# Gates turned and spread over the adapter ranks through DRAM, so that the down projection of the middle chunks is made transposed

## The chip, the cores and the metric

The kernel runs on one NeuronCore of one Trainium2 chip. The metric is the device time of one execution in microseconds. A core has TensorE (PE), which multiplies matrices into PSUM; VectorE (DVE), ScalarE (ACT) and GpSimd (POOL) for elementwise work; SyncE (SP), which issues transfers; and 16 DMA engines that all queues share.

## The reference

Two stages are computed, attention over a pooled key grid and then a mixture of eight small adapters on its output:

```
kv_pool = kv.reshape(B, H/4, 4, W/4, 4, C).mean(axis=(2, 4))   # B 4, C 128: 768 keys a batch
k = v = kv_pool.reshape(B, -1, C) @ w_sr
a = softmax((q @ k.T) / sqrt(C));  x = a @ v                    # q: 12288 rows a batch
logits = x @ w_gate                                             # 8 experts
top 2 of 8 -> softmax over the two -> w
out = x + sum over the two experts e of  w_e * (x @ A[e]) @ B[e]   # rank 16
```

All eight experts are computed for every row: eight experts of rank 16 are 128 columns, and experts that weren't chosen have gate 0. With two chosen experts the softmax is a sigmoid of the difference of logits, which the kernel makes with a tanh; the factor of one half is folded into A.

## The kernel before, in words

**Tiling.** The 4 x 12288 query rows are cut into 96 chunks of T = 512 rows (24 per batch, `NB`); a chunk is S = 4 blocks of 128 rows. Groups of four chunks (`GC`) share one load of queries: `cast_q` (L79) casts 2048 rows to bf16 in DRAM on GpSimd's queue, `load_qT` (L84) reads them back transposed on the sync queue.

**One chunk** goes through these steps, each a function of its own:

- `scores` (L311): for r = 0, 1, 2 two matmuls of 512 columns into a two-bank PSUM tile `sg`, then one exponential on ScalarE (L319) to `em` in fp16. The pool of `sg` has two buffers.
- `attend` (L321): for each of the four row blocks six matmuls of 137 columns into `acc`: 128 value columns, 8 gate logits (w_gate is folded into the values) and the sum of the exponentials. `acc` has one buffer.
- `normalize` (L331): reciprocal and product on VectorE give `xn`.
- `top` (L362) and `route` (L371): the eight sorted logits on VectorE; differences and mask on GpSimd. Chunks are routed in pairs (`sizes`).
- `gates` (L389): a tanh on ScalarE, a product and a sum on GpSimd give `gw`.
- `transposes` (L398): turns `xn` of one chunk and the gated activations `hg` of another by matmul with the identity, four matmuls each, into one tile `tt_ps`; one copy on VectorE takes both out (L416).
- `down` (L422): four matmuls per chunk with the turned x as weights and A (`a_bf`) as the moving operand give rows by (expert, rank).
- `gate` (L427): VectorE multiplies by the gate of the row and expert, read 16 times over along the rank, into `hg`.
- `up` (L436): four matmuls with the turned `hg` as weights; `finish` (L441): VectorE adds `xn`, and the sync queue stores.

**Order.** The order on every engine is the program's order. Chunks up to 13 and the stretch from chunk 72 on follow order strings written out by hand; slots 14 to 71 come from `slot(k)` (L646). In slot k the kernel computes scores of chunk k, attends for k-1, normalizes k-2, gates k-4 (once per pair), runs the down projection of k-6, turns x of k-6 and `hg` of k-7, and finishes k-8. The slot's core in the code:

```
o.append(f"sc {k} 0")
...
o += [f"nm {k - 2}", f"tt {k - 6} {k - 7} V", f"sc {k} 1", f"up {k - 8}", f"fi {k - 8}",
      f"at {k - 1} 0", f"tp {k - 2}"]
...
o += [f"sc {k} 2", f"dn {k - 6}", f"ge {k - 6}"]
```

**Keys of the next batch.** `load_kv` loads 12 pieces of 512 KB per batch in 12 slots running, GpSimd adds them up (`pa`), and nine steps (`pr`: keys, values, turn, for each third) bring them to `kfT` and `vx`. `next_cast` (L605) first makes GpSimd touch the last query tile that was loaded, so that a cast starts after that load.

**PSUM.** `sg` takes two banks in each of its two buffers, `acc` takes two, and the other products (`tt_ps`, `h_ps`, `d_ps`, the keys' tiles) share a pool of two banks called mb.

Of the kernel before, what the change touches and what calls it, by code (L numbers as in the profile page):

```python
# [20 lines left out]
def kernel(  # L21
# [10 lines left out]
    nc = tc.nc  # L32
    P = 128
    B, N, C = q.tensor.shape
    E, RK = 8, 16
# [3 lines left out]
    T = 512  # L39
    S = T // P  # L40
    GC = 4
# [7 lines left out]
    const = ctx.enter_context(tc.tile_pool(name="const", bufs=1))  # L49
# [6 lines left out]
    rpool = ctx.enter_context(tc.tile_pool(name="rpool", bufs=4))  # L56
    gpool = ctx.enter_context(tc.tile_pool(name="gpool", bufs=6))
    run = ctx.enter_context(tc.tile_pool(name="run", bufs=3))
    opool = ctx.enter_context(tc.tile_pool(name="opool", bufs=6))
    qdram = ctx.enter_context(tc.tile_pool(name="qdram", bufs=1, space=bass.MemoryType.DRAM))  # L60
    ps_s = ctx.enter_context(tc.tile_pool(name="ps_s", bufs=2, space=bass.MemoryType.PSUM))
    ps_a = ctx.enter_context(tc.tile_pool(name="ps_a", bufs=1, space=bass.MemoryType.PSUM))
# [2 lines left out]
    keep = tc.keep_in_program_order  # L65

    def mm(*a, **k):
        return keep(nc.tensor.matmul(*a, **k))  # L68

    def mtile(shape, dtype=FP32, name="mb"):  # L70
        return ps_m.tile(shape, dtype, tag="mb", name=name)


    NG = N // GT
# [48 lines left out]
    for item in """  # L123
# [5 lines left out]
        at = [None if x == "-" else int(x) for x in at]  # L129
# [13 lines left out]
    id_f = const.tile([P, P], FP32)  # L143
# [163 lines left out]
    em, acc, xn, xg, srt, gw = {}, {}, {}, {}, {}, {}  # L307
    tts, xT, hgT, hp, hg, dp = {}, {}, {}, {}, {}, {}
# [34 lines left out]
    def normalize_half(k, h):  # L343
        if ("r", k) not in xn:
            xn["r", k] = rpool.tile([P, S], FP32, tag="rinv", name="rinv")
        if k // GC not in xg:
# [5 lines left out]
            xn[k][:, 2 * h:2 * h + 2], a[:, :, 0:VC],  # L352
            ri.unsqueeze(2).broadcast_to([P, 2, VC]), op=ALU.mult)))

    sizes = [1, 1] + [2] * (NB * (B - 1) // 2 - 1) + [1] * NB
    first, size = {}, {}
    for n in sizes:
        k0 = len(first)
# [3 lines left out]
    def top(k):  # L362
        k0, m = first[k], k - first[k]
        if k0 not in srt:
            srt[k0] = rpool.tile([P, GC, S, 8], FP32, tag="srt", name="srt")
        for s in range(S):
            keep(nc.vector.max(srt[k0][:, m, s], xn[k][:, s, C:VC]))  # L367

# [2 lines left out]
    def route(k0):  # L371
        n = size[k0] * S
        eng = nc.gpsimd
        m0 = k0 % GC * S
        lg = xg[k0 // GC].rearrange("p m s c -> p (m s) c")[:, m0:m0 + n, C:VC]
        so = srt[k0].rearrange("p m s e -> p (m s) e")[:, 0:n]

        def over(i):
            d = rpool.tile([P, GC * S, 8], FP32, tag=f"over{i}", name=f"over{i}")[:, 0:n]
            keep(eng.tensor_tensor(  # L380
                d, lg, so[:, :, i].unsqueeze(2).broadcast_to([P, n, 8]), op=ALU.subtract))
            return d

        arg, mask = over(0), over(1)
        keep(eng.tensor_tensor(arg, arg, mask, op=ALU.add))
        keep(eng.tensor_scalar(mask, mask, 0.0, None, op0=ALU.is_ge))  # L386
        routed[k0] = (n, eng, arg, mask)

    def gates(k0):  # L389
        n, eng, arg, mask = routed[k0]  # L390
        th = rpool.tile([P, GC * S, 8], FP32, tag="th", name="th")[:, 0:n]
        keep(nc.scalar.activation(th, arg, AF.Tanh, bias=0.0, scale=0.5))  # L392
        w = gpool.tile([P, GC * S, 8], FP32, tag="gw", name="gw")
        keep(eng.tensor_tensor(w[:, 0:n], th, mask, op=ALU.mult))  # L394
        keep(eng.tensor_tensor(w[:, 0:n], w[:, 0:n], mask, op=ALU.add))  # L395
        gw[k0] = w
# [30 lines left out]
    def gate(k):  # L427
        k0, m = first[k], k - first[k]
        hg[k] = run.tile([P, S, P], BF16, tag="hg", name="hg")
        keep(nc.vector.tensor_tensor(  # L430
            hg[k].rearrange("p s (e r) -> p (s e) r", e=E),
            hp[k].rearrange("p s (e r) -> p (s e) r", e=E),
            gw[k0][:, m * S:(m + 1) * S].rearrange("p s e -> p (s e)")
            .unsqueeze(2).broadcast_to([P, S * E, RK]), op=ALU.mult))

    def up(k):  # L436
        dp[k] = mtile([P, S, C], name="d_ps")
        for s in range(S):
            mm(dp[k][:, s], hgT[k][:, s], b_bf, start=(s == 0), stop=(s == S - 1))
# [146 lines left out]

    def gates_here(k):
        th, mask = routed[k]
        gw[k] = gpool.tile([P, S, E], FP32, tag="gw1", name="gw1")
        keep(nc.vector.scalar_tensor_tensor(gw[k], th, 1.0, mask, op0=ALU.add, op1=ALU.mult))  # L590

    late = const.tile([P, 1], FP32)
    a_bf = const.tile([P, P], BF16)
    b_bf = const.tile([P, C], BF16)

    def adapters():
        keep(nc.vector.tensor_scalar(a_bf, a_f, 0.5, None, op0=ALU.mult))
        keep(nc.vector.tensor_copy(b_bf, b_f))

    def first_casts(watch):  # L600
        keep(nc.gpsimd.tensor_copy(late, watch))
        for g in range(2, 4):
            cast_q(g)
# [7 lines left out]
    def plan(b):  # L611
# [20 lines left out]
        "nh": normalize_half, "xb": hold_x, "xt": turn_x, "cx": fetch_x, "hb": hold_h, "ht": turn_h, "ch": fetch_h,  # L632
        "o95": hold_acc, "pt": attend_part, "hd": hold_hp, "dn2": down_into, "ge2": gate_part,
        "db": hold_d, "up2": up_part, "af": add_here, "ca": carry, "pd": add_there,
        "lastroute": route_here, "lt": tanh_here, "lg_": gates_here,
    }

    def follow(order):
# [7 lines left out]
    def slot(k):  # L646
        b, i = divmod(k, NB)
        o = []
        if k % GC == 0 and k // GC + 1 < B * NG:
            o.append(f"lq {k // GC + 1}")  # L650
        i0 = 4 if b == 0 else 0
        if b + 1 < B and i0 <= i < i0 + 12:
            o.append(f"kv {b + 1} {(i - i0) // 4} {(i - i0) % 4}")
        if k % GC == 2 and k // GC + 2 < B * NG:
            o.append(f"cq {k // GC + 2}")
        o.append(f"sc {k} 0")
        if first[k - 4] == k - 4:
            o.append(f"ga {k - 4}")
        o += [f"nm {k - 2}", f"tt {k - 6} {k - 7} V", f"sc {k} 1", f"up {k - 8}", f"fi {k - 8}",
              f"at {k - 1} 0", f"tp {k - 2}"]  # L660
        if first[k - 2] + size[k - 2] - 1 == k - 2:
            o.append(f"ro {first[k - 2]}")
        o += [f"sc {k} 2", f"dn {k - 6}", f"ge {k - 6}"]
        prs = (14, 15, 16, 18, 19, 20, 21, 22, 23) if b == 0 else (11, 12, 13, 17, 18, 19, 21, 22, 23)
        if b + 1 < B and i in prs:
            o.append(f"pr {b + 1} {prs.index(i)}")
        o += [f"at {k - 1} {s}" for s in range(1, S)]
        if b + 1 < B and i % 2 == 0 and (8 if b == 0 else 6) <= i <= 20:
            lo, n = ((0, 3, 7, 10, 14, 17, 21)[(i - 8) // 2], 4 if i % 4 else 3) if b == 0 else (
                (i - 6) // 2 * 3, 3)  # L670
            o += [f"pa {b + 1} {m}" for m in range(lo, lo + n)]
        return "; ".join(o)

    follow("""
# [26 lines left out]
    for k in range(14, 72):  # L701
        follow(slot(k))
# [89 lines left out]
```

The softmax here doesn't subtract the row's maximum and nothing guards it: scores larger than these inputs give would overflow.

## Time and profile before

| | |
|---|---|
| time, median of 3 runs | 389.32 us (lowest 388.84) |
| span of the profiled run | 387.5 us, TensorE clock 0.998 |
| PE busy | 378.9 us, 98% |
| VectorE, ScalarE, GpSimd busy | 81%, 80%, 54% |
| moved by DMA | 76.5 MB |
| one exponential (L319), 288 of them | 1026 ns |
| store of one chunk, issue to landing | 3.3 us |
| load of one key piece, issue to landing | 6.2 us |

How to read it: a line of a group has the source line, engine and operation, what is written from what, the shape and the count; after the bar follow busy microseconds, the mean of one in nanoseconds, and the engine's idle time before it with what ended that. A helper records all matmuls, so they all carry L68 and are told apart by their tiles. Matmuls overlap in the pipeline, so the distance between two starts, not the duration, tells what one occupies. In a timeline the columns are start and length in microseconds.

### The profile page before, as it was taken

Reading aid. Unit: us, or ns where it says so; the run is one execution under the profiler, and the core shown is the slowest. Engines: PE = TensorE matmul, PEld = TensorE weight load, DVE = VectorE, ACT = ScalarE, POOL = GpSimd, SP = SyncE. Lnnn points to the kernel's source line nnn. Section 1 sums busy time; section 2 is a strip of 40 time slices with the busy share of each in tenths; the row PEclk is TensorE's granted clock in tenths of the full one; section 3 lists DMA queues with packets and bytes.
Section 4 is the critical chain, followed back from the end, with each engine's and each line's share of the span. In section 5 each row is a group of like instructions: output and inputs, shape, how many; then the busy total and the mean of one; then the engine's idle time right before and its main releaser. Section 6 shows DMA issues by size and latency. Waiting matters only on the chain.

```text
span 387.5 us, 11812 instructions
## 1 busy us (share of the span) xinstructions
PE 378.9 (98%) x4620; PEld 303.8 (78%) x4620; DVE 313.5 (81%) x973; ACT 308.3 (80%) x401; POOL 211.0 (54%) x474
## 2 busy tenths in 40 slices
PE   7899999999999999999999999999999999999994
PEld 4777788888888887888887887888877778788893
DVE  1445688989888888989988889888877687988896
ACT  1688997777687786877788787786879999998964
POOL 0011768987331768777533586877613234545682
PEclk9999999999999999999999999999999999999999
DMA  7998997975596999985579989856745665532245
GB/s 263 413 267 200 295 201 220 285 164 140 136 314 140 255 227 331 234 172 142 119 191 272 305 206 333 200 138 142 156 113 105 128 150 165 111 92 105 81 165 219
DMA packets 70745, 76.47 MB, mean 197 GB/s; under 512 B 49857, under 2 KB 51393, under 8 KB 70337
## 3 DMA queue, kind: packets, MB, share of 16 engines
q1 hardware_dynamic: 69552, 63.98, 55.8%
q0 software_dynamic: 704, 11.54, 17.1%
q8 instruction: 36, 0.59, 0.6%
q10 hardware_dynamic: 432, 0.20, 0.2%
q14 instruction: 21, 0.16, 0.2%
HBM read 50.53 MB, written 36.70 MB: 225 GB/s over the span
## 4 chain that ended last, share of the span: by engine, by line
PE 82%; DMA 8%; POOL 5%; DVE 1%; ACT 1%; issue 1%; SPq 0%; POOLq 0%; DVEq 0%; ACTq 0%
PE acc L68 32%; PE sg L68 29%; PE tt_ps L68 8%; DMA kvr<-in_kv_dram 6%; PE h_ps L68 4%; PE d_ps L68 3%; PE tail_ps L68 3%; DMA qT<-qbf 2%; POOL osb L562 1%; PE v_ps L68 1%; POOL over L380 1%; PE kpT_ps L68 1%; POOL gw L394 1%; ACT em L319 1%; POOL gw L395 1%
## 5 line engine op out<-in xcount | busy, mean ns | idle before, releaser
L319 ACT ACTIVATE em<-sg 128x1024 f16<-128x1024 f32 x288 | 278.3, 1026 | 56.4 <-PE sg L68 55.9
L68 PE MATMUL sg<-qT,kfT 128*128 128x512 bf16 x576 | 169.6, 379 | 0.0
L68 PE MATMUL acc<-vx,em 128*128 128x137 f16 x2280 | 168.9, 223 | 0.0
L68 PEld LDWEIGHTS <-em 128*128 128x128 f16 x2304 | 147.2, 98 | 11.4 <-DVE xn L337 2.7
L68 PEld LDWEIGHTS <-tts 128*128 128x128 bf16 x660 | 49.2, 98 | 31.8 <-issue 0.2
L264 POOL TENSOR_TENSOR kvr<-kvr 128x512 f32<-128x512 f32 x54 | 67.4, 1271 | 0.0
L337 DVE TENSOR_TENSOR xn<-acc,rinv 128x544 f32<-128x544 f32 x83 | 60.1, 724 | 3.2 <-DVE rinv L333 0.3
L380 POOL TENSOR_TENSOR over<-xn,srt 128x64 f32<-128x64 f32 (+1 forms) x114 | 29.8, 282 | 55.2 <-DVE srt L367 55.2
L416 DVE COPY tts<-tt_ps 128x1024 bf16<-128x1024 bf16 (+1 forms) x83 | 53.9, 651 | 4.8 <-PE tt_ps L68 4.6
L394 POOL TENSOR_TENSOR gw<-th,over 128x64 f32<-128x64 f32 (+1 forms) x57 | 16.7, 293 | 63.7 <-ACT th L392 62.7
L68 PEld LDWEIGHTS <-kfT 128*128 128x128 bf16 x576 | 46.1, 98 | 2.8
L430 DVE TENSOR_TENSOR hg<-h_ps,gw 128x512 bf16<-128x512 f32 x58 | 40.1, 691 | 4.5
L68 PEld LDWEIGHTS <-xn 128*128 128x128 bf16 x384 | 28.6, 98 | 18.2
L443 DVE TENSOR_TENSOR osb<-d_ps,xn 128x512 f32<-128x512 f32 x58 | 40.1, 691 | 0.0
L333 DVE RECIPROCAL rinv<-acc 128x4 f32<-128x4 f32 x83 | 15.1, 182 | 29.3 <-PE acc L68 28.6
L68 PE MATMUL tt_ps<-id_bf,xn 128*128 128x128 bf16 x344 | 33.3, 219 | 0.0
L367 DVE MAX8 srt<-xn 128x8 f32<-128x8 f32 x368 | 33.0, 152 | 0.1
L68 PE MATMUL tt_ps<-id_bf,hg 128*128 128x128 bf16 x316 | 30.4, 219 | 0.0
L68 PEld LDWEIGHTS <-hg 128*128 128x128 bf16 x384 | 25.6, 98 | 1.9 <-DVE hg L531 0.3
L68 PE MATMUL h_ps<-a_bf,tts 128*128 128x128 bf16 x264 | 25.5, 219 | 0.0
L68 PE MATMUL d_ps<-b_bf,tts 128*128 128x128 bf16 x260 | 25.1, 219 | 0.0
L386 POOL TENSOR_SCALAR over<-over 128x64 f32<-128x64 f32 (+1 forms) x57 | 19.1, 335 | 5.2
(119 smaller groups left out, 325.3 us busy)
## 6 DMA issues: line engine op xcount, KB each, us to landing
out_dram<-osb SPq DMA_DIRECT2D x91, 256.0 KB, 3.3
kvr<-in_kv_dram SPq DMA_DIRECT2D x45, 512.0 KB, 6.2
qbf<-in_q_dram POOLq DMA_DIRECT2D x22, 512.0 KB, 6.3
kvr<-in_kv_dram SPq DMA_DIRECT2D x6, 256.0 KB, 8.6
out_dram<-osb SPq DMA_DIRECT2D x9, 128.0 KB, 2.1
qf<-in_q_dram SPq DMA_DIRECT2D x4, 256.0 KB, 6.9
qf<-in_q_dram SPq DMA_DIRECT2D x2, 512.0 KB, 8.2
qT<-qbf SPq DMA_TRANSPOSE x22, 5.1
```

The costliest lines, as they stand in the source:

```text
L68: return keep(nc.tensor.matmul(*a, **k))
L264: keep(nc.gpsimd.tensor_tensor(u[:, lo:hi], u[:, lo:hi], v[:, lo:hi], op=ALU.add))
L319: keep(nc.scalar.activation(em[k][:, 2 * r:2 * r + 2], ps, AF.Exp, bias=0.0, scale=scale))
L333: keep(nc.vector.reciprocal(ri, acc[k][:, :, VC]))
L337: keep(nc.vector.tensor_tensor(x, acc[k][:, :, 0:VC], ri.unsqueeze(2).broadcast_to([P, S, VC]), op=ALU.mult))
L367: keep(nc.vector.max(srt[k0][:, m, s], xn[k][:, s, C:VC]))
L380: keep(eng.tensor_tensor(d, lg, so[:, :, i].unsqueeze(2).broadcast_to([P, n, 8]), op=ALU.subtract))
L386: keep(eng.tensor_scalar(mask, mask, 0.0, None, op0=ALU.is_ge))
L394: keep(eng.tensor_tensor(w[:, 0:n], th, mask, op=ALU.mult))
L416: keep(nc.vector.tensor_copy(sb[:, lo:hi], ps[:, lo:hi]))
L430: keep(nc.vector.tensor_tensor(hg[k].rearrange("p s (e r) -> p (s e) r", e=E), hp[k].rearrange("p s (e r) -> p (s e) r", e=E), gw[k0][:, m ...
L443: keep(nc.vector.tensor_tensor(osb, dp[k], xn[k][:, :, 0:C], op=ALU.add))
```

## The change

For the 48 chunks 14 to 61 (24 pairs, `turned`) the down projection is made the other way round. A is the weight operand and the turned x the moving one, so that one matmul of 512 columns gives (expert, rank) by rows; its product with the gates is at once the turned `hg` which `up` needs as weights, and the turn of `hg` falls away. For that the gates are needed with (expert, rank) on the partitions. GpSimd writes them as fp16; per pair one matmul turns them to (expert, chunk, block) by row, VectorE copies them out, one transfer puts them into DRAM as 8 rows of 1024, and another reads each row back 16 times, onto 128 partitions. The turned chunks run two slots later in the adapter part (x turned in slot k+8, up in slot k+9).

Besides, key loads come every second slot instead of in 12 slots running, the query cast no longer waits for the last query load and stands after the gates in its slot, and the query load stands behind the spreading of gates in the sync queue.

```diff
+    gxpool = ctx.enter_context(tc.tile_pool(name="gxpool", bufs=3))
+    gdram = ctx.enter_context(tc.tile_pool(name="gdram", bufs=4, space=bass.MemoryType.DRAM))
...
+    turned = {*range(14, 62),}
...
     def gates(k0):
...
+        if k0 in turned:
+            keep(eng.tensor_tensor(th, th, mask, op=ALU.mult))
+            gh[k0] = gpool.tile([P, E, n], FP16, tag=f"gh{n}", name="gh")
+            keep(eng.tensor_tensor(gh[k0].rearrange("p e m -> p m e"), th, mask, op=ALU.add))
+            return
...
+    def turn_gates(k0, pool, engine):
+        n = size[k0] * S * E
+        ps = one(pool).bitcast(FP16)[0:n, 0:P]
+        mm(ps, gh[k0].rearrange("p e m -> p (e m)"), id_h, is_transpose=True, start=True, stop=True)
+        gt[k0] = rpool.tile([P, P], FP16, tag="gt", name="gt")[0:n]
+        move(engine, gt[k0], ps)
+
+    def put_gates(k0):
+        gd[k0] = gdram.tile([E, size[k0] * T], FP16, tag=f"gd{size[k0]}", name="gd")
+        keep(nc.sync.dma_start(gd[k0].rearrange("e (m t) -> (e m) t", t=P), gt[k0]))
+
+    def spread_gates(k0):
+        n = size[k0] * T
+        gx[k0] = gxpool.tile([P, GC // 2 * T], FP16, tag="gx", name="gx")[:, 0:n]
+        keep(nc.sync.dma_start(gx[k0], gd[k0].unsqueeze(1).broadcast_to([E, RK, n])))
+
+    def down_turned(k, pool):
+        hp[k] = one(pool)
+        mm(hp[k], a_bf, xT[k].rearrange("p s t -> p (s t)"), start=True, stop=True)
+
+    def gate_turned(k):
+        m = k - first[k]
+        hgT[k] = run.tile([P, S, P], BF16, tag="hg", name="hg")
+        keep(nc.vector.tensor_tensor(hgT[k].rearrange("p s t -> p (s t)"), hp[k],
+                                     gx[first[k]][:, m * T:(m + 1) * T], op=ALU.mult))
...
     def slot(k):
         b, i = divmod(k, NB)
         o = []
-        if k % GC == 0 and k // GC + 1 < B * NG:
-            o.append(f"lq {k // GC + 1}")
-        i0 = 4 if b == 0 else 0
-        if b + 1 < B and i0 <= i < i0 + 12:
-            o.append(f"kv {b + 1} {(i - i0) // 4} {(i - i0) % 4}")
-        if k % GC == 2 and k // GC + 2 < B * NG:
-            o.append(f"cq {k // GC + 2}")
+        n, rest = divmod(k + 8, 2)
+        if k < 16:
+            o.append(f"kv 1 2 {k - 12}")
+        elif rest == 0 and n % 12 + 12 * (n // 12 - 1) < 12 * (B - 2):
+            o.append(f"kv {n // 12 + 1} {n % 12 // 4} {n % 4}")
         o.append(f"sc {k} 0")
         if first[k - 4] == k - 4:
             o.append(f"ga {k - 4}")
-        o += [f"nm {k - 2}", f"tt {k - 6} {k - 7} V", f"sc {k} 1", f"up {k - 8}", f"fi {k - 8}",
-              f"at {k - 1} 0", f"tp {k - 2}"]
+        if k % GC == 2 and k // GC + 2 < B * NG:
+            o.append(f"cr {k // GC + 2}")
+        o.append(f"nm {k - 2}")
+        far, near = k - 8 in turned, k - 6 not in turned
+        x = k - 6 if near else "-"
+        h = "-" if k - 7 in turned else k - 7
+        if (x, h) != ("-", "-"):
+            o.append(f"tt {x} {h} V")
+        if far:
+            o.append(f"tt {k - 8} - V")
+        o.append(f"sc {k} 1")
...
+            o += [f"up {j}", f"fi {j}"]
+        if first[k - 6] == k - 6 and k - 6 in turned:
+            o.append(f"g3 {k - 6}")
+        if k % GC == 0 and k // GC + 1 < B * NG:
+            o.append(f"lq {k // GC + 1}")
+        o.append(f"at {k - 1} 0")
+        o.append(f"tp {k - 2}")
...
+        o.append(f"sc {k} 2")
+        if far:
+            o += [f"dT {k - 8} mb", f"gT {k - 8}"]
+        if near:
+            o += [f"dn {k - 6}", f"ge {k - 6}"]
...
-        o += [f"at {k - 1} {s}" for s in range(1, S)]
...
+        o += [f"at {k - 1} {s}" for s in range(1, S - 1)]
+        if first[k - 4] == k - 4 and k - 4 in turned:
+            o += [f"g1 {k - 4} mb V", f"g2 {k - 4}"]
+        o.append(f"at {k - 1} {S - 1}")
```

The short names stand for `turn_gates` (g1), `put_gates` (g2), `spread_gates` (g3), `down_turned` (dT), `gate_turned` (gT) and a bare `cast_q` (cr). The pooling steps of the first batch (`pa`) are laid out over a few more slots.

More of the change, by code (lines that the diff above doesn't have):

```diff
@@ L353, in normalize_half @@
             ri.unsqueeze(2).broadcast_to([P, 2, VC]), op=ALU.mult)))
+    turned = {*range(14, 62),}
+    gh, gt, gd, gx = {}, {}, {}, {}
+    id_h = const.tile([P, P], FP16)
     sizes = [1, 1] + [2] * (NB * (B - 1) // 2 - 1) + [1] * NB
@@ L364, in top @@
         if k0 not in srt:
-            srt[k0] = rpool.tile([P, GC, S, 8], FP32, tag="srt", name="srt")
+            srt[k0] = rpool.tile([P, 2, S, 8], FP32, tag="srt", name="srt")
         for s in range(S):
@@ L378, in over @@
         def over(i):
-            d = rpool.tile([P, GC * S, 8], FP32, tag=f"over{i}", name=f"over{i}")[:, 0:n]
+            d = rpool.tile([P, 2 * S, 8], FP32, tag=f"over{i}", name=f"over{i}")[:, 0:n]
             keep(eng.tensor_tensor(
@@ L390, in gates @@
         n, eng, arg, mask = routed[k0]
-        th = rpool.tile([P, GC * S, 8], FP32, tag="th", name="th")[:, 0:n]
+        th = rpool.tile([P, 2 * S, 8], FP32, tag="th", name="th")[:, 0:n]
         keep(nc.scalar.activation(th, arg, AF.Tanh, bias=0.0, scale=0.5))
-        w = gpool.tile([P, GC * S, 8], FP32, tag="gw", name="gw")
+        if k0 in turned:
[3 more added lines that the diff above has]
+            return
+        w = gpool.tile([P, 2 * S, 8], FP32, tag="gw", name="gw")
         keep(eng.tensor_tensor(w[:, 0:n], th, mask, op=ALU.mult))
@@ L588, in gates_here @@
         th, mask = routed[k]
+        if k in turned:
+            gh[k] = gpool.tile([P, E, S], FP16, tag=f"gh{S}", name="gh")
+            keep(nc.vector.scalar_tensor_tensor(gh[k].rearrange("p e m -> p m e"), th, 1.0, mask, op0=ALU.add, op1=ALU.mult))
+            return
         gw[k] = gpool.tile([P, S, E], FP32, tag="gw1", name="gw1")
@@ L598, in adapters @@
         keep(nc.vector.tensor_copy(b_bf, b_f))
+        keep(nc.vector.tensor_copy(id_h, id_f))
     def first_casts(watch):
@@ L634 @@
         "db": hold_d, "up2": up_part, "af": add_here, "ca": carry, "pd": add_there,
-        "lastroute": route_here, "lt": tanh_here, "lg_": gates_here,
+        "cr": cast_q, "g1": turn_gates, "g2": put_gates, "g3": spread_gates, "dT": down_turned,
+        "gT": gate_turned, "lastroute": route_here, "lt": tanh_here, "lg_": gates_here,
     }
@@ L658, in slot @@
             o.append(f"ga {k - 4}")
-        o += [f"nm {k - 2}", f"tt {k - 6} {k - 7} V", f"sc {k} 1", f"up {k - 8}", f"fi {k - 8}",
-              f"at {k - 1} 0", f"tp {k - 2}"]
+        if k % GC == 2 and k // GC + 2 < B * NG:
[9 more added lines that the diff above has]
+        o.append(f"sc {k} 1")
+        done = []
+        if k - 8 not in turned:
+            done.append(k - 8)
+        if k - 9 in turned:
+            done.insert(0, k - 9)
+        for j in done:
+            o += [f"up {j}", f"fi {j}"]
[5 more added lines that the diff above has]
+        o.append(f"tp {k - 2}")
         if first[k - 2] + size[k - 2] - 1 == k - 2:
             o.append(f"ro {first[k - 2]}")
-        o += [f"sc {k} 2", f"dn {k - 6}", f"ge {k - 6}"]
+        o.append(f"sc {k} 2")
[3 more added lines that the diff above has]
+            o += [f"dn {k - 6}", f"ge {k - 6}"]
         prs = (14, 15, 16, 18, 19, 20, 21, 22, 23) if b == 0 else (11, 12, 13, 17, 18, 19, 21, 22, 23)
@@ L666, in slot @@
             o.append(f"pr {b + 1} {prs.index(i)}")
-        o += [f"at {k - 1} {s}" for s in range(1, S)]
[L668 to L671, printed above, removed]
+        o += [f"at {k - 1} {s}" for s in range(1, S - 1)]
+        if first[k - 4] == k - 4 and k - 4 in turned:
+            o += [f"g1 {k - 4} mb V", f"g2 {k - 4}"]
+        o.append(f"at {k - 1} {S - 1}")
+        if b + 1 < B:
+            adds = {14: (10, 13), 15: (13, 14), 16: (14, 17), 17: (17, 18), 18: (18, 21),
+                    20: (21, 24)} if b == 0 else {
+                        6 + 2 * n: (3 * n, 3 * n + 3) for n in range(8)}
+            if i in adds:
+                o += [f"pa {b + 1} {m}" for m in range(*adds[i])]
         return "; ".join(o)
```

## The prediction

> **What bounds the kernel now.** First the page's busy shares and its chain of waits.
>
> ```profile
> PE 378.9 (98%) x4620; PEld 303.8 (78%) x4620; DVE 313.5 (81%) x973; ACT 308.3 (80%) x401; POOL 211.0 (54%) x474
> ...
> PE 82%; DMA 8%; POOL 5%; DVE 1%; ACT 1%; issue 1%; SPq 0%; POOLq 0%; DVEq 0%; ACTq 0%
> ```
>
> TensorE is busy for 98% of the span and is 82% of the chain. A modelled busy time can hide gaps, so next come the windows (busy time by stage) and then the timeline of one slot of the steady stage, where PE start times can be subtracted.
>
> ```profile
> 100.00:150.00 50.00, 49.90 (x631) 40.33 (x630) 43.59 (x127) 39.56 (x47) 24.88 (x55) 1.00 0.91 230
> 200.00:250.00 50.00, 50.00 (x632) 40.28 (x631) 44.23 (x127) 39.72 (x48) 29.79 (x62) 1.00 0.97 273
> ```
>
> Here PE leaves nothing free at full clock; VectorE has 12 to 13% left, ScalarE 21%. The last two columns are the DMA share, 0.91 and 0.97, and GB/s. The timeline of slot 36, PE first, then ScalarE:
>
> ```profile
> 149.88 0.59 PE L68 MATMUL sg<-qT,kfT 128*128 128x512 bf16 x2
> 150.31 0.39 PE L68 MATMUL tt_ps<-id_bf,xn 128*128 128x128 bf16 x4
> 150.53 0.39 PE L68 MATMUL tt_ps<-id_bf,hg 128*128 128x128 bf16 x4
> 150.75 0.59 PE L68 MATMUL sg<-qT,kfT 128*128 128x512 bf16 x2
> 151.19 0.39 PE L68 MATMUL d_ps<-b_bf,tts 128*128 128x128 bf16 x4
> 151.41 0.52 PE L68 MATMUL acc<-vx,em 128*128 128x137 f16 x6
> 151.77 0.59 PE L68 MATMUL sg<-qT,kfT 128*128 128x512 bf16 x2
> 152.20 0.39 PE L68 MATMUL h_ps<-a_bf,tts 128*128 128x128 bf16 x4
> ...
> 154.02 0.38 PE L68 MATMUL sg<-qT,kfT 128*128 128x512 bf16 x1
> ```
>
> ```profile
> 150.57 1.02 ACT L319 ACTIVATE em<-sg 128x1024 f16<-128x1024 f32 x1 [1.31 <-PE sg L68]
> ```
>
> Starts give what one matmul occupies: four of 128 columns take 150.53 - 150.31 = 0.22 us (0.055 each), two of 512 take 0.43 (0.215 each), six of 137 take 0.36 (0.06 each). A slot without key preparation is 16 x 0.055 + 6 x 0.215 + 24 x 0.06 = 3.61; slot starts in the trace are 3.63 apart. So PE has no gap, and work taken off it is time, **until another chain closes**. That chain is in these lines. The pool for sg has two buffers, so the slot's third score group may start only when the first exponential has ended: 150.57 + 1.02 = 151.59. It starts at 151.77, 0.18 later. How close can it come? The trace has a stretch where ScalarE is the bound:
>
> ```profile
> 303.76 0.59 PE L68 MATMUL sg<-qT,kfT 128*128 128x512 bf16 x2
> 304.67 0.59 PE L68 MATMUL sg<-qT,kfT 128*128 128x512 bf16 x2
> 305.59 0.59 PE L68 MATMUL sg<-qT,kfT 128*128 128x512 bf16 x2
> ```
>
> Score groups follow each other every 0.917 us there, each 0.051 us after the end of the exponential two before it; over all 288 groups that is the smallest distance, reached 15 times. The slack in the steady slot is therefore 0.18 - 0.05 = 0.127 us.
>
> **What the Trainium skill says.** "TensorE: Matmul & The Clock Gate", Back-to-back issue gap, gives 56 and 216 ns for isolated matmuls of 128 and 512 columns, and about 81 and 131 ns as sustained; the trace has 55 and 215 ns in a sustained stream, so I use those. "DMA: Bandwidth & Descriptors" has three statements that matter. Issuing engines are not separate DMA queues: casts, stores and loads share 16 DMA engines; the trace agrees, the median store lands after 5.8 us at 100 to 150 us, beside key loads, and 3.3 at 150 to 200. Two DMAs through the same engine are not ordered: the reader's issuer must wait for the writer's semaphore; no run here shows it yet. Anatomy of one DMA puts about 2.0 us of fixed cost on a transfer (for GpSimd's path); the fastest store here lands after 1.9.
>
> **The change part by part.** PE, for each of the 48 chunks 14 to 61: eight 128-column matmuls go (four turns of hg, four of the down projection), 8 x 0.055 = 0.444 with the exact 0.0555; one of 512 comes, 0.216; half a turn of the gates comes, 0.028. That is 0.200 less, and 48 x 0.200 = **9.6 us**.
>
> *Where in the slot it falls.* The built order shows, between first and second score group, four transposes where there were eight: 0.22 less. The rest (up, six attends, then the down projection and 18 attends) keeps its length. So the third group would be reached at 0.43 + 0.22 + 0.43 + 0.22 + 0.36 = 1.67 after the first; the first exponential starts 0.69 after it, as now (ScalarE idles before it in either case), ends at 1.71 and lets the group go at 1.766. PE waits 0.095 us (0.222 - 0.127). Slots 20 and 23 to 67 are such: 46 x 0.095 = **4.4 us back**. In slots 21 and 22 the longer pipeline (x two slots later, up one later) leaves out four more matmuls each: 0.317 of wait, together **0.6**. The work so deferred comes in slots 68 to 70, which serve old and new form at once. VectorE has about 3.9, 4.6 and 4.6 us there against 3.8, 4.3 and 4.4 of PE: some 0.6 short with 0.3 to 0.4 of slack: **0.3**.
>
> VectorE otherwise gains (groups by shape; after the bar busy us and mean ns):
>
> ```profile
> L416 DVE COPY tts<-tt_ps 128x1024 bf16<-128x1024 bf16 x71 | 49.0, 691 | 3.6 <-PE tt_ps L68 3.5
> L430 DVE TENSOR_TENSOR hg<-h_ps,gw 128x512 bf16<-128x512 f32 x58 | 40.1, 691 | 4.5
> L416 DVE COPY tts<-tt_ps 128x512 bf16<-128x512 bf16 x12 | 4.9, 419 | 1.2 <-PE tt_ps L68 1.1
> ```
>
> The copy goes from 691 to 419 ns, the gate product has the same shape (691), and a gate copy of 64x128 per pair comes (no row; between 166, the 128x8 copy, and 293, the 128x128 fp32 copy, both from PSUM; I take 220). Net 0.16 less per chunk, hidden by PE; so is the one cast of the identity to fp16 (about 0.22, like that of b_bf). One place is tight: attend needs acc, freed when xn is normalized at 1.14 in the slot; the shortest usual distance from xn to attend is 0.17, so 1.31, just when PE arrives (1.53 now, less 0.22). A few ns lost there only fill the 0.095.
>
> GpSimd keeps its number of gate operations (320 ns each). The fp16 store is unpriced: from nothing to a doubling, 0.32. It ends 2.73 us into the slot, and the turn of the gates waits for it at 1.77 + 0.43 + 0.22 + 0.72 = 3.13; both ends fit, I take nothing. Behind that turn six attends and the next scores queue. Casts lose their wait for qT (8.4 us of GpSimd idle); this helps the pooling that makes PE wait 0.27 and 0.16 us at kpT_ps. The shorter slot takes about as much from the pooling's lead: nothing net. Spread key loads cost no engine and halve that part of the DMA load; the gates add 24 x (256 + 16) KB = 6.7 MB to 76.5.
>
> *The new wait.* Per pair: gates written at the end of slot K+4, read back in K+6, used 2.6 us into K+8. From issue of the read, some 2.9 into its slot, to use is 2 x 3.52 - 0.3 = 6.8 us. The read has the bytes of a store: 1.9 at best, 3.3 to 5.8 by median, 11.0 at worst (in a burst at 130 us). I take 5: hidden. If late, VectorE stops at the gate product; the next normalization queues behind it, and PE waits for acc.
>
> Sum: 389.3 - 9.6 + 4.4 + 0.6 + 0.3 = **385.0 us**.
>
> **The rivals.** *Full gain:* the exponential closes earlier, or its wait is taken up elsewhere, and the 9.6 come whole: 379.7. For it: PE's lack of any gap. Against it: the 0.051 us floor and the fixed 0.69 + 1.02. *Late gates, slower:* the sync queue is serial, and a qT load in it waits for its cast:
>
> ```profile
> SPq L84 <- DMA qbf<-in_q_dram: 45.7, 13, 9.6
> ```
>
> That is the waits of the DMA queue: us in total, times, longest. It waits up to 9.6 us and then issues for up to 4.8 (SP timeline, 120.93). Every second gate write stands behind such a load, and its read behind that write's landing. A wait for the cast to 4.8, issue to 9.6, landing at 12 to 13.5 put the read at 13 to 14 and its data at 17 to 19, against use at 16.7, all counted from that slot's start. With 12 such pairs late by 1.5 us: 385.0 + 18 = 403. In half-bad cases (0.3 to 0.75 us) it gives 389 to 394. Against it: with a cast landing in 6 us and a 2.9 us issue, the data are there near 15. *ScalarE as the bound outright:* 3 x 0.917 + 0.125 = 2.88 per slot, under 3.49: no case.
>
> **How the numbers follow.** My forecast 0.62 (384 to 387); half-bad lateness 0.18 (387 to 394); late gates 0.12 (397 and more); full gain 0.08 (under 381.5). The range leaves out the last two: 381 to 394. Faster by over 2% means under 381.5: 0.09 with a margin; slower means over 397.1: 0.12; within: 0.79.
>
> **What would show it.** Right: slots 23 to 67 at 3.49 and 3.55 in turn, third score group 0.05 after the first exponential and 1.77 after the first group, PE waiting some 0.1 there; matmuls down by 312. Wrong: idle time of VectorE at the gate product released by gx (late gates), PE waiting for gh, or slots near 3.42 (full gain).

## The result, and the profile after

The changed kernel takes 406.16 us (median of 4 runs, 404.74 to 407.88) against 389.09 for the kernel before on the same chip: ratio 1.044, 95% interval 1.038 to 1.051. It is slower. Medians here and below are over all executions, while ratios and their intervals leave out the slow ones, those over 1.5% above the fastest of the same kernel. The profiled run spans 402.9 us, before 387.5. The page of after, the lines that answer to those of before (busy shares, two DMA queues, the chain by engine and by line, one group):

```profile
PE 382.1 (95%) x4308; PEld 291.4 (72%) x4308; DVE 304.5 (76%) x999; ACT 310.3 (77%) x401; POOL 209.4 (52%) x459
...
q1 hardware_dynamic: 74736, 70.66, 60.8%
q0 software_dynamic: 704, 11.54, 16.3%
...
PE 60%; DMA 24%; POOL 5%; DVE 5%; issue 2%; ACT 2%; SPq 1%; POOLq 0%; DVEq 0%; ACTq 0%
PE acc L70 23%; PE sg L70 22%; DMA gx<-gd 17%; PE tail_ps L70 6%; PE tt_ps L70 4%; DMA qT<-qbf 3%; PE d_ps L70 2%; DMA kvr<-in_kv_dram 2%; DMA gd<-gt 2%; DVE hg L469 2%; POOL osb L598 1%; ACT em L321 1%; PE h_ps L70 1%; PE v_ps L70 1%; POOL over L385 1%
...
L469 DVE TENSOR_TENSOR hg<-tail_ps,gx 128x512 bf16<-128x512 f32 x48 | 33.2, 692 | 26.3 <-DMA gx<-gd 17.6
```

The 312 matmuls are gone (4620 to 4308), yet the chain that ended last has moved from PE (82% to 60%) to transfers (8% to 24%), 17 of the 24 to one of them: gates read back from DRAM (gx). VectorE stands idle 17.6 us at the gate product (L469) for it. The waits view, VectorE and then PE (us in total, times, longest), shows who pays:

```profile
DVE hg L469 <- DMA gx<-gd: 17.6, 9, 4.0
```

```profile
PE tt_ps L70 <- DVE hg L469: 6.7, 6, 1.7
PE tail_ps L70 <- DVE hg L469: 4.2, 2, 3.5
```

Where it happens: all nine late reads belong to pairs whose first chunk divides by four, the ones whose gate write stands behind a query load. Slots 33, 36, 57 and 60 last 5.38, 4.96, 5.18 and 8.09 us, where undisturbed slots last 3.49 (odd) and 3.77 (even). Here is one, PE and then VectorE in the timeline of after (start, length, and in brackets the idle time before):

```profile
139.33 0.59 PE L70 MATMUL sg<-qT,kfT 128*128 128x512 bf16 x2
141.64 0.38 PE L70 MATMUL tt_ps<-id_bf,xn 128*128 128x128 bf16 x4 [1.72 <-DVE hg L469]
```

```profile
140.90 0.69 DVE L469 TENSOR_TENSOR hg<-tail_ps,gx 128x512 bf16<-128x512 f32 x1 [2.85 <-DMA gx<-gd]
```

VectorE is in order: the product waits for gx, the next normalization waits behind the product, and PE, which could go on at 139.33 + 0.43 = 139.76, goes on at 141.64. The read that it waited for is the last line of this stretch of the sync queue's timeline:

```profile
125.37 4.53 SPq L86 DMA_TRANSPOSE qT<-qbf  x1
129.99 0.54 SPq L455 DMA_DIRECT2D gd<-gt  x1
130.62 0.54 SPq L480 DMA_DIRECT2D out_dram<-osb  x1
...
132.53 0.61 SPq L460 DMA_DIRECT2D gx<-gd  x1
```

It was issued at 132.53, in a slot that began at 128.30, so 4.2 into it where the prediction had 2.9. Its data were used at 140.90, the moment the wait ended: 8.4 us from issue, where the prediction took 5. What the read met on the engines is in the DMA view of 132 to 141 us (queue: packets, MB, share of the 16 engines' time):

```profile
q1 hardware_dynamic: 764, 1.59, 52.6%
q0 software_dynamic: 32, 0.52, 36.2%
```

Queue q0 carries the query casts alone. One cast takes 36% of these 9 us, or 3.3 us of all 16 engines, between the read's issue and its use. So two things coincide in the pairs whose first chunk divides by four: their gate write stands behind a query load, and their read is issued in the slot of a cast. The reads of the other 12 pairs have no cast in between, and none of them is late. The late issue is the queue's order, the long landing the engines' load. Which one matters is what the experiments ask.

One more thing is in the timeline, in a slot with no wait (slot 30, even, PE and then ScalarE):

```profile
128.30 0.59 PE L70 MATMUL sg<-qT,kfT 128*128 128x512 bf16 x2
...
130.07 0.59 PE L70 MATMUL sg<-qT,kfT 128*128 128x512 bf16 x2
130.50 0.38 PE L70 MATMUL tail_ps<-tts,a_bf 128*128 128x512 bf16 x1
130.71 0.88 PE L70 MATMUL acc<-vx,em 128*128 128x137 f16 x12
131.53 0.24 PE L70 MATMUL tail_ps<-id_h,gh 128*64 128x128 f16 x1
131.70 0.53 PE L70 MATMUL acc<-vx,em 128*128 128x137 f16 x6
132.07 0.38 PE L70 MATMUL sg<-qT,kfT 128*128 128x512 bf16 x1
```

```profile
128.99 1.02 ACT L321 ACTIVATE em<-sg 128x1024 f16<-128x1024 f32 x1 [0.76 <-PE sg L70]
```

The third score group starts 1.77 after the first and 0.06 after the exponential's end, as forecast. But the turn of the gates costs more than its 0.055: the twelve attends before it need 12 x 0.06 = 0.72 and get 0.82, and the next attend starts 0.17 after it. The 64-column weight load (128\*64) does not hide behind the matmuls around it. Over the trace the gap before it has a median of 0.153 and it occupies 0.176; with about 0.01 on the attend that follows, a pair loses some 0.22 against the forecast, and 24 pairs 5.3 us.

### The profile page after: what moved, and what is told of

It is laid out like the page before. It is cut to its first block, busy times and chain, and to the rows that moved or that the text cites. A ratio compares the mean times of both kernels' runs of the same rounds, so it can differ in the third digit from the quotient of the medians.

```text
span 402.9 us, 11319 instructions
## 1 busy us (share of the span) xinstructions
PE 382.1 (95%) x4308; PEld 291.4 (72%) x4308; DVE 304.5 (76%) x999; ACT 310.3 (77%) x401; POOL 209.4 (52%) x459
## 3 DMA queue, kind: packets, MB, share of 16 engines
q1 hardware_dynamic: 74736, 70.66, 60.8%
q0 software_dynamic: 704, 11.54, 16.3%
## 4 chain that ended last, share of the span: by engine, by line
PE 60%; DMA 24%; POOL 5%; DVE 5%; issue 2%; ACT 2%; SPq 1%; POOLq 0%; DVEq 0%; ACTq 0%
PE acc L70 23%; PE sg L70 22%; DMA gx<-gd 17%; PE tail_ps L70 6%; PE tt_ps L70 4%; DMA qT<-qbf 3%; PE d_ps L70 2%; DMA kvr<-in_kv_dram 2%; DMA gd<-gt 2%; DVE hg L469 2%; POOL osb L598 1%; ACT em L321 1%; PE h_ps L70 1%; PE v_ps L70 1%; POOL over L385 1%
## 5 line engine op out<-in xcount | busy, mean ns | idle before, releaser
L70 PE MATMUL acc<-vx,em 128*128 128x137 f16 x2280 | 173.5, 223 | 0.0
L70 PEld LDWEIGHTS <-em 128*128 128x128 f16 x2304 | 148.2, 98 | 25.6 <-issue 4.4
L469 DVE TENSOR_TENSOR hg<-tail_ps,gx 128x512 bf16<-128x512 f32 x48 | 33.2, 692 | 26.3 <-DMA gx<-gd 17.6
L426 DVE COPY tts<-tt_ps 128x512 bf16<-128x512 bf16 (+1 forms) x84 | 40.6, 487 | 5.0 <-PE tt_ps L70 4.8
L70 PEld LDWEIGHTS <-hg 128*128 128x128 bf16 x384 | 27.9, 98 | 14.3 <-issue 1.5
L404 POOL TENSOR_TENSOR gw<-th,over 128x32 f32<-128x32 f32 (+1 forms) x33 | 9.1, 276 | 44.2 <-ACT th L397 43.1
L70 PEld LDWEIGHTS <-tts 128*128 128x128 bf16 x276 | 19.7, 98 | 9.2 <-issue 0.6
L399 POOL TENSOR_TENSOR th<-th,over 128x64 f32<-128x64 f32 x24 | 7.7, 320 | 33.5 <-ACT th L397 33.5
L390 POOL TENSOR_TENSOR over<-over,over 128x64 f32<-128x64 f32 (+1 forms) x57 | 16.7, 293 | 4.5
L70 PE MATMUL d_ps<-b_bf,hg 128*128 128x128 bf16 x192 | 18.7, 221 | 0.2
```

The source lines that it names most:

```text
L426: keep(nc.vector.tensor_copy(sb[:, lo:hi], ps[:, lo:hi]))
L469: keep(nc.vector.tensor_tensor(hgT[k].rearrange("p s t -> p (s t)"), hp[k], gx[first[k]][:, m * T:(m + 1) * T], op=ALU.mult))
```

## The experiments

Theories: **queue order** (gate transfers stand behind the query load in the sync queue; a better order saves all), **one slow read** (only the gates' read is late; take away its consumer and all comes back), and **capacity** (the 16 DMA engines have no room for the gates beside keys, queries and stores; some transfer is late whatever the order). All times are medians; each ratio is against runs of the kernel before on the same chip, at 388.8 to 389.1.

### Who waits, and in what order

**Gates from a constant, transfers kept.**

```diff
-                                     gx[first[k]][:, m * T:(m + 1) * T], op=ALU.mult))
+                                     gfix, op=ALU.mult))
```

> The gate product of the turned chunks reads a constant tile (0.25) in place of the spread gates; the turn of the gates, both transfers and everything else stay, so only the wait for the read-back is gone. The experts' share of these chunks is therefore made with wrong gates. Theory late gates: adding up by how much slots 28 to 65 of the changed kernel exceed their neighbours gives some 15 us of PE standing behind VectorE's wait for gx, so 391 us (389 to 393). Rival traffic: the added transfers hold up queries and keys, whoever reads the gates: stays at 400 us or above.

Measured: 405.87 us, ratio 1.041 (1.037 to 1.045). Nobody reads gx, and nothing is gained. The waits of PE in this run:

```profile
PE sg L70 <- DMA qT<-qbf: 8.8, 3, 4.3
PE sg L70 <- DMA kvr<-in_kv_dram: 1.5, 2, 1.0
```

The wait has moved to the next transfer that someone needs, the query load, for which the waits view of the kernel before shows no wait of PE. These 8.8 us are less than the 15 that were to come back; part of the rest is the clock, 0.990 in the mean here and 0.998 before, some 3 us of 401 (see the last section). "One slow read" falls.

**Query load behind the gate write.** The step `lq` moves behind `g1`, `g2` in its slot.

> The query load of a slot stands behind the slot's write of the gates in the sync queue, no longer ahead of it; nothing else moves. Theory sync queue: the gate write and all behind it are late because the query load issues for 4 to 4.5 us ahead of them; with it behind, gates come in time, 391 to 394 us. Rival cast: the gates' read-back is late because a query cast, one 32 KB packet per DMA engine for 2.4 to 4 us, runs just ahead of it; then little changes, 402 us or above.

Measured: 406.18 us, 1.043 (1.039 to 1.047). VectorE waits for gx 25.3 us in 12 places, more than before the move.

**Cast in the next slot.** The step `cr` moves from the gates of slot k with k % 4 = 2 to the start of the one after.

> The query cast is issued one slot later, at the start of slot 4g+3, and not behind the gates of slot 4g+2 where the read-back of a pair's gates is issued at the same time; nothing else moves. Theory cast: the read-back goes ahead of the cast and lands in time, 391 to 395 us. Rival sync queue: the order in the queue is what it was, so 402 us or above.

Measured: 406.03 us, 1.044 (1.040 to 1.048); gx waits 18.0 us.

**Stores issued by ScalarE.**

```diff
+        if k in turned:
+            held.append((k, osb))
+            return
...
+        for k, osb in held:
+            keep(nc.scalar.dma_start(dest(k), osb))
...
+        o.append("st")
```

> The stores of the turned chunks are issued by ScalarE at the end of their slot, where it is idle for 0.6 us, and not by the sync queue; bytes and packets are the same. Theory DMA capacity: no gain, 402 to 410 us. Rival sync queue: one issue of 0.3 to 0.6 us and one wait for VectorE per slot leave the queue, gates and queries go out earlier, 390 to 397 us.

Measured: 406.88 us, 1.043 (1.037 to 1.048). The waits of VectorE for gates and of PE for exponentials in this run:

```profile
DVE hg L469 <- DMA gx<-gd: 10.6, 5, 2.9
```

```profile
PE sg L70 <- ACT em L321: 4.5, 4, 3.4
```

The gates wait less (10.6 us for 17.6), but PE now waits for exponentials, a wait that the changed kernel doesn't show. ScalarE takes its work in order, and in its timeline an idle stretch of 4.3 us ends with the issue of a store at 155.31 and an exponential at 155.75. So this run gains nothing, but it doesn't show what a relieved sync queue alone would bring. "Queue order" as the sole cause falls with the first two: neither move of a step gained anything.

**Gates turned with 128 weight columns.** They are written into the first 64 columns of a cleared tile, the matmul loads all 128, and only the wanted rows are copied out.

```diff
-        mm(ps, gh[k0].rearrange("p e m -> p (e m)"), id_h, is_transpose=True, start=True, stop=True)
+        mm(ps, wide[k0 // 2 % 6], id_h, is_transpose=True, start=True, stop=True)
...
-        move(engine, gt[k0], ps)
+        move(engine, gt[k0], ps[0:n])
```

> The turn of the gates loads 128 weight columns (64 of gates, 64 zeros from a buffer cleared once) where it had 64. In the changed kernel this one matmul lengthens its slot by 0.28 us and not 0.055. Theory narrow weights: a load of fewer than 128 columns isn't overlapped, so 24 x 0.22 = 5 us go: 401 us. Rival wait: the load isn't overlapped because it waits for GpSimd: stays within 2 us of 406.

Measured: 407.17 us, 1.049 (1.045 to 1.052). PE's timeline in this run:

```profile
131.53 0.88 PE L70 MATMUL acc<-vx,em 128*128 128x137 f16 x12
132.25 0.22 PE L70 MATMUL tail_ps<-id_h,wide 128*128 128x128 f16 x1
132.30 0.46 PE L70 MATMUL acc<-vx,em 128*128 128x137 f16 x5
```

131.53 to 132.25 is 0.72, the plain twelve attends, and the turn occupies 0.05; over all 24 pairs the gap before it has a median of 0.060 and it occupies 0.056. So the cause of PE's extra 0.22 per pair is the weight load of 64 columns. The Trainium skill, "TensorE: Matmul & The Clock Gate", Weight-path perf modes, says that the fast weight load is on for 128 weights; that the slow load here is this mode's absence fits, but no run here shows the mode itself. The time does not follow (it stays within 2 us of 406, the number of the rival): VectorE's wait for gx is 20.1 us where it was 17.6. In this run what PE saves is given back in a longer wait for a transfer.

### Less traffic

**Constant gates, and 1/16 of each read-back.** The read moves 64 of 1024 columns: 24 x 240 KB = 5.9 MB less.

```diff
-        keep(nc.sync.dma_start(gx[k0], gd[k0].unsqueeze(1).broadcast_to([E, RK, n])))
+        keep(nc.sync.dma_start(gx[k0][:, 0:64], gd[k0][:, 0:64].unsqueeze(1).broadcast_to([E, RK, 64])))
```

> As e1 (constant gates, so the experts' share of the turned chunks is wrong), and each read-back moves 64 of its 1024 columns: the same number of transfers in the same order, 24 x 240 KB less traffic. Theory DMA capacity: in the changed kernel all 16 DMA engines are busy for 0.92 of 100 to 260 us while 39 chunks pass, 3.7 us per chunk, more than the 3.5 that TensorE would need; a read-back costs 128 packets x 0.084 / 16 = 0.67 us of that per pair, so 0.31 per chunk go here, TensorE is the bound again and the time is 390 us (388 to 392: the forecast of 385 and 5 us for the slow turn of the gates). Rival sync queue: the count and order of issues is what holds things up; stays at 402 us or above.

Measured: 390.99 us (390.68 to 391.34), 1.005 (1.003 to 1.006). Against the constant gates alone only bytes were taken away, and 14.9 us come back. What is left is the forecast's sum with the turn of the gates put right: 385.0 + 5.3 = 390.3.

**A quarter of each store.** Turned chunks store one of four row blocks; gates are whole.

> Gates complete and waited for, but each turned chunk stores one of its four row blocks (the other rows of the output stay unwritten): 48 x 192 KB less traffic, the same number of transfers in the same order. Theory DMA capacity: whose bytes go doesn't matter; 0.5 us per chunk go, 390 us (388 to 392), and the wait for gx nearly vanishes. Rival gates: the read-back of one 16 KB region of DRAM 16 times over is slow by itself; the wait for gx and the time stay, 400 us or above.

Measured: 394.8 us, 1.015 (1.013 to 1.016). Bytes of another stream, whose landing nobody near waits for, bring 11.4 us. The time stays above the 388 to 392 us expected, since the gates are still late:

```profile
DVE hg L469 <- DMA gx<-gd: 9.2, 9, 2.7
```

**The same with both order changes** (query load behind the gate write, cast in the next slot).

> As e8 (one of four row blocks of a turned chunk stored, the others stay unwritten), and the order of e2 and e3 on top: the query load behind the gate write, the cast one slot later. e8 came to 394.8 us and still had 9.2 us of waits for gx. Theory order: with room on the engines, what is left of the lateness comes from the order, 390 to 392 us and under 4 us of waits for gx. Rival: the rest is capacity too, within 1 us of 394.8.

Measured: 392.73 us, 1.010 (1.008 to 1.011), gx waits 3.8 us in 2 places. Once there is room the order is worth 2.1 us; without room (above) it was worth nothing.

### Traffic without a waiter

**Nothing turned.** `turned = set()`: key loads stay spread, the order stays new, gates take the old way.

> No chunk is turned: the part of the change that spreads the key loads, moves the query load behind the stores and frees the cast of its wait, alone. Theory DMA capacity: without the gates' traffic there are some 3.2 us of DMA per chunk against 3.63 of TensorE: 389 us, within 1. Rival order: the spread loads, or casts that run beside transposed loads, are what hurts; 395 us or more.

Measured: 389.07 us, 1.000 (0.9995 to 1.0014). The three moves together (spread keys, query load, cast) neither cost nor bring anything by themselves.

**The transfers alone.** On top of that the same two transfers per pair, 16 KB out and 256 KB in, from data that is there at any time, into a tile that nobody reads; then the same with two reads.

```diff
+        for _ in range(1):
+            x = gxpool.tile([P, T], FP32, tag="gx", name="gx")
+            rows = q[0, 0:4 * E].rearrange("(e r) c -> e (r c)", e=E)
+            keep(nc.sync.dma_start(x, rows.unsqueeze(1).broadcast_to([E, RK, T])))
```

> As e7 (no chunk turned, all gates made as before), and for each of the 24 pairs the same two transfers stand in the sync queue at the same places: a 16 KB write of the identity to DRAM and a read of 16 KB of q, 16 times over, into a tile that nobody reads. No engine computes more, and nobody waits for them. Theory DMA capacity: e7 needs 0.88 x 160 / 43 = 3.27 us of all DMA engines per chunk, the two transfers add 0.42, together 3.7 beside TensorE's 3.72: no room left, 395 to 405 us. Rival waiting: what costs is that VectorE waits for the gates; 389 us, within 2.

> As e13 with two such reads per pair. Theory DMA capacity: 4.05 us of DMA per chunk against 3.72, so the time follows the traffic, by 0.35 x 48 = 17 us over e13: 410 to 422 us. Rival waiting: still 389 to 393 us.

Measured: 398.13 us for the single traffic, scattered from 393.43 to 404.31, ratio 1.014 (1.011 to 1.018). Twice the reads: 424.88 us, 1.091 (1.089 to 1.094), above the 410 to 422 expected. PE's waits in the latter:

```profile
PE sg L70 <- DMA qT<-qbf: 25.6, 8, 6.0
```

Transfers that no instruction needs stop PE, through the query loads that share the engines with them; with nothing turned and no such transfers PE waits 0.2 us for queries. The waits of 25.6 us and the mean clock of 0.970 instead of 0.998, some 12 us of 423, together account for about the 35.8 us between the two runs. The added transfers also occupy the sync queue, which is issuing for 153 of the 160 us from 100 to 260 us by its timeline (136 with nothing turned), so this run alone doesn't tell the engines from the queue that issues. The short read does: there the issues stayed and only bytes went.

The windows from 100 to 260 us show it as a balance. The columns are busy us and instructions of PE, PE loads, VectorE, ScalarE, GpSimd; clock; DMA share; GB/s. First before:

```profile
100.00:260.00 160.00, 159.90 (x2011) 129.22 (x2010) 141.08 (x408) 125.36 (x150) 95.42 (x190) 1.00 0.85 220
```

After:

```profile
100.00:260.00 160.00, 149.12 (x1592) 108.74 (x1590) 121.32 (x392) 116.81 (x138) 84.92 (x164) 0.99 0.92 231
```

Short read:

```profile
100.00:260.00 160.00, 158.42 (x1709) 117.95 (x1736) 134.45 (x429) 125.84 (x152) 95.30 (x181) 1.00 0.89 214
```

Short stores:

```profile
100.00:260.00 160.00, 155.62 (x1676) 115.62 (x1703) 130.96 (x420) 123.88 (x148) 92.40 (x178) 1.00 0.81 194
```

Double traffic:

```profile
100.00:260.00 160.00, 138.10 (x1633) 109.53 (x1631) 114.78 (x330) 102.33 (x122) 72.36 (x142) 0.94 0.99 234
```

The exponentials in the window (129, 119, 130, 127, 105, three per chunk) give the chunks done. Share x 160 / chunks is the time all 16 DMA engines are busy per chunk: 3.16, 3.71, 3.29, 3.06 and 4.53 us. PE needs 3.72 per chunk before (160 / 43). With the matmuls of the changed kernel it needs 3.69: that is the pace of the short read (160 / 43.3), where PE is busy for 158.42 of 160 us. Before, the engines have 0.56 us to spare per chunk; after, 3.71 stands against 3.69 and nothing is left. Two cautions. The trace doesn't say how much of a packet's busy time is waiting, so this need not be pure demand. And the mean doesn't foretell lateness: short stores have the lowest share of all and still wait 9.2 us for gates, each time beside a cast (see "Not settled" below).

### Can part of the gain be kept?

**Short read with both mends**: constant gates, 1/16 of the read, 128 weight columns, and the down projection with its gate product ahead of the third score group (`dT`, `gT` before `sc k 2`), which fills the 0.095 us wait. (The tile of the gates has two buffers here, not three.)

> As e5 (constant gates, short read-backs), and the two costs that e5 still has on TensorE are taken away: the gates are turned as 128 weight columns (e4), and a turned chunk's down projection stands ahead of the slot's third score group, so that the group is reached 1.88 us after the first and no longer waits for the exponential. The experts' share of the turned chunks is wrong as in e5. Theory: 24 x 0.22 = 5.3 and 46 x 0.095 + 2 x 0.2 = 4.8 us go from 391.0: 381 us (380 to 383), near the 379.7 of the full gain. Rival: ScalarE or VectorE close another chain, 386 us or above.

Measured: 386.36 us, 381.67 to 399.0 over 12 runs; ratio 0.990 (0.988 to 0.993). By the ratios the mends bring 5.6 us of the 10 hoped for (1.005 to 0.990). The number is that of the rival, but no other chain has closed: in the profile (an execution of 389.43 us) the undisturbed slots last 3.40 (odd) and 3.45 us (even), where the short read has 3.49 and 3.77, so there the mends work in full. What is missing in it is two query loads that came late:

```profile
PE sg L70 <- DMA qT<-qbf: 6.0, 2, 4.3
```

The fastest execution, 381.67 us, lies within the 380 to 383 expected. So even with 1/16 of each read, transfers are at times late.

**Fewer pairs.** Same mends, full gates, key loads in 12 slots running as before, and only chunks 30 to 41 and 54 to 61 turned (10 pairs), mostly where no keys are loaded; then 26 to 43 and 50 to 61 (15 pairs).

```diff
-    turned = {*range(14, 62),}
+    turned = {*range(30, 42), *range(54, 62)}
```

> The whole computation. 20 chunks are turned and not 48: 30 to 41 and 54 to 61, whose gates are read back in slots 36 to 47 and 60 to 67, where no keys are loaded, since the key loads are put back into 12 slots running; with the wide turn and the early down projection of e9. Theory DMA capacity: before, such stretches had a DMA share of 0.54 to 0.78, so the gates fit in, and 20 x 0.200 less some 0.8 for the two ends is 3.2 us: 386 us, faster than both kernels. Rival order: gates are late behind query loads and casts whatever the share is: 390 us or above.

> As e10 with 30 chunks turned, 26 to 43 and 50 to 61: the gates of 5 more pairs are read back beside key loads, where the DMA share before was 0.9 to 1.05. Theory DMA capacity: 30 x 0.200 less 0.8 would give 383.9, but some of the five pairs find the engines full and are late: 384 to 388 us, no better than e10 by more than 2. Without any limit by DMA: 383.9 us.

Measured: 391.18 us, 1.007 (1.004 to 1.009) for 10 pairs; 399.62, 1.027 (1.025 to 1.030) for 15. With 10 pairs VectorE waits 2.0 us for gx, with 15 pairs:

```profile
DVE hg L472 <- DMA gx<-gd: 11.5, 5, 5.4
```

Five pairs more, placed beside key loads, cost 8.4 us. But 10 pairs don't pay either, and the 2.0 us of waiting explain that only in part: 20 chunks should have saved about 20 x 0.2 = 4. More is in the trace, if the start of each chunk's first exponential is set beside that of the kernel before. The two turned stretches get ahead by 2.2 us up to slot 48 and by 1.6 more up to slot 68, and the three slots after each (48 to 50, 68 to 70) give back 1.7 and 2.3, with no wait for gx among them. Part of that is work which the start of the stretch only put off; how much is loss wasn't separated, but the 0.8 us that the expectation gave the two ends was too little. No version that computes everything beat the kernel before.

## Why the prediction was wrong

- **PE's removed work and ScalarE's limit: right.** Odd slots last 3.491 us (forecast 3.49); the third score group starts 1.767 after the first (1.77) and 0.051 after the exponential; 312 matmuls fewer; gate product 692 ns (691), copy of half size 416 (419), gate copy 212 to 216 (220).
- **The half turn of the gates at 0.028 per chunk: mis-sized.** It is 0.28 per pair instead of 0.055, hence even slots of 3.77 instead of 3.55. The term is -9.6 + 5.3. The prediction took the price of a matmul of 128 weight columns for one with 64; the wide turn shows that the columns are the reason. GpSimd's fp16 store, 479 ns instead of 320, stayed hidden as assumed.
- **Slots 68 to 70, with 0.3 us for VectorE: mis-sized.** The prediction gave them 3.8, 4.3 and 4.4 us of PE and 0.3 of waiting, 12.8 in all. In the short read they last 4.06, 5.41 and 4.72 between first exponentials, 14.2. The total still came out, since slots 23 to 67 there take 1.1 us less than before, where 3.49 and 3.77 in turn against 3.63 would make them the same; that the two nearly cancel is luck.
- **"The new wait ... I take 5: hidden": the step that failed.** The read was issued 1.3 us later than taken and landed in 8.4 instead of 5. Behind it stands the step before it: "Spread key loads cost no engine ...; the gates add 24 x (256 + 16) KB = 6.7 MB to 76.5" was a price of zero for the DMA engines, in a text whose own windows show them at 0.91 and 0.97. The short read shows the size of the error: 405.9 - 391.0 = 14.9 us.
- **The sum put right:** 385.0 + 5.3 + 14.9 = 405.2, measured 406.16. Only the first two terms were worked out; the 14.9 is the measured difference of two runs, so this sum shows where the time is and not that it could have been foretold.
- **The rival "late gates"** foretold 403 us and the symptom: VectorE stopped at L469, every second pair, PE behind it. Its mechanism, a gate write behind the query load, is seen in the queue's timeline, but putting it right brought nothing until bytes were removed, and then 2.1 us together with the cast. The size agrees by luck: its own cause accounts for a small part.
- **Not settled: how much of the lateness is the query cast.** By the page of after the cast queue has 704 packets and 11.54 MB. Half of them are of 32 KB, 16 to a cast, and take 0.163 x 16 x 402.9 / 352 = 3.0 us each (the other half hold 4 bytes); those of the main queue take 0.608 x 16 x 402.9 / 74736 = 0.05. All nine late reads of after, and all nine of the short stores, have a cast between issue and use. In the short stores, where the 2 KB packets of the main queue are gates alone, a read beside a cast starts to move 4.4 us after its issue and ends after 6.7, one without a cast 1.5 and 3.9 (medians of 11 and 10 reads, from chunk 20 on). Moving the cast by a slot changed nothing, but it didn't part the two: in the trace of that run the five reads that are late by over 2 us still have a cast in between, with 2.1 to 3.4 us of all engines. A version with smaller casts, or without casts, wasn't tried.
- **Not tried: a wider read.** In the short stores a gates' read has at most 8 packets under way for 93% of its time, where stores of the kernel before reach 16 and more. It looks as if the read used half of the engines; one laid out for all 16 might land sooner.

## What to carry to other kernels

In this kernel, whose DMA engines were busy for 0.85 of the steady stage, transfers that nobody waits for still cost time. So before adding one, work out engine time per unit of work beside PE's time per unit, before and after, and take the landing times of transfers in that stage's bursts, not medians. If removing a wait only moves it to the next transfer, as here from the gates to the queries, count bytes before reordering further. PE time saved here while transfers were late came back as waiting (the wide turn), so such savings were seen only with the traffic taken away. And count the slots in which an old and a new form overlap: after the stretches of 10 pairs they gave back all of the lead.

## What the hardware showed besides

**A wait can cost more than its length.** In slot 60 of after PE stands idle 3.47 us for late gates. These are one-us windows of after (the column before the DMA share is the granted clock):

```profile
253.00:254.00 1.00, 0.00 (x0) 0.00 (x0) 0.00 (x0) 0.00 (x0) 1.00 (x1) 1.00 0.87 341
254.00:255.00 1.00, 0.09 (x1) 0.00 (x0) 0.84 (x3) 0.00 (x0) 0.07 (x1) 0.95 0.25 98
255.00:256.00 1.00, 1.00 (x8) 0.82 (x8) 0.67 (x3) 0.00 (x0) 0.00 (x0) 0.50 0.19 64
256.00:257.00 1.00, 1.00 (x6) 0.53 (x5) 0.91 (x2) 0.07 (x1) 0.00 (x0) 0.50 0.58 210
257.00:258.00 1.00, 1.00 (x6) 0.45 (x4) 0.42 (x1) 0.95 (x1) 0.00 (x0) 0.50 0.71 154
```

The clock falls to half as the wait ends and is 0.84 in the window after these: some 3.4 us at half (254.9 to 258.3), which is another 1.7 us lost. The Trainium skill describes it in "TensorE: Matmul & The Clock Gate", What's actually happening: half clock after an idle window of about 3.4 us, full clock again after a busy one. The trace agrees in both lengths. The double traffic pays it repeatedly: its mean clock over the run is 0.970, where before has 0.998.

**A weight load of 64 columns is dearer than one of 128** in a running stream: 0.28 us against 0.055 for the same 128-column matmul.
